# A guarded fallback rewritten as nested loops, and the warm-up matmuls of the opening cut in two

## Chip, cores and metric

One core of one Trainium2 chip. The metric is device time in microseconds of one execution. The kernels compared in one job ran on the same chip in turns.

## The reference

```python
# x, f_logit: (4, 6080, 256); lower_bound: (256,); w_in: (256, 2048); w_out: (2048, 256)
f = lower_bound + (1 - lower_bound) * sigmoid(f_logit)
for t in range(S):                       # a recurrence along the sequence
    h = f[:, t] * h + (1 - f[:, t]) * x[:, t]
    y[:, t] = h
z = y.reshape(B * S, D) @ w_in           # 24320 x 2048
out = (z - tanh(z)) @ w_out
```

## The kernel before

It has two paths. The fast one works on blocks of 512 tokens, uses an approximation of z - tanh(z) that holds for small z, and writes down whether any z was too large (`flags`, summed up into `flag`). Only if one was, a slower path computes everything again.

```python
    fast()
    seen = nc.values_load(flag[:].bitcast(INT32), ...)
    with tc.If(seen != 0):
        general()                       # the path for large h
```

The opening of the fast path has to wait for the first transfers. To get the clock of TensorE up meanwhile, it multiplies zeros (the spares), in four groups of 7, 4, 4 and 2 that stand at fixed places of the instruction order. TensorE is called cold where a matmul of 512 columns takes 0.427 us from start to start, and warm where it takes 0.217; the prediction reads both from the trace.

```python
        def keep_busy(n):
            for _ in range(n):
                nc.tensor.matmul(
                    busy[:], lhsT=zeros.bitcast(BF16)[:, 0:P],
                    rhs=zeros.bitcast(BF16)[:, 0:TB], start=True, stop=True,   # TB = 512
                    skip_group_check=True,
                )
        before = """
            K1.7 df.0 ce.0 ...  sg0.0 cb.0 K1.4
            sg1.0 df.1 ...      F.0.0.0 f0.1 v1.1 f1.1 dx.2 v0.1 K1.4 cw.1
            t.0.0.0 sc0.1 q.0.0.0 F.0.0.1 w.0.0.0 W.3 sc1.1 cr.2 K1.2 a.0.0.0 t.0.0.1
            F.1.0.0 ...                                    # [cut]
```

`K1.n` is a group of n spares, `F.*` the products of the first layer, `sc*` the recurrence on VectorE, `cw.*` the end of a weight's conversion from float64. In the profiles below, `A`, `B`, `D` and `Qa` to `Qd` are the accumulators that a matmul writes, `y` is the recurrence's result, and line 673 holds transposes. The path for large h, before the change, is one loop over time with the four units of 512 hidden columns written out:

```python
        with tc.For_i(0, S, H) as t0:            # 190 steps
            ...                                  # [cut] loads, recurrence
                ps = ps_o.tile([P, D], FP32, name="psO")[0:nb]
                for u in range(NU):              # unrolled: 4 x 12 products
                    for s in range(2):
                        ...                      # 4 products w_in, tanh, 2 products w_out
                nc.scalar.copy(out=osb[0:nb], in_=ps)
```

Of the kernel before, what the change touches and what calls it, by code (L numbers as in the profile page):

```python
# [9 lines left out]
FP32 = mybir.dt.float32  # L10
ALU = mybir.AluOpType
# [4 lines left out]
BF16 = mybir.dt.bfloat16  # L16
PSUM = bass.MemoryType.PSUM
P = 128
# [13 lines left out]
def kernel(  # L32
# [25 lines left out]
    nc = tc.nc  # L58

    B, S, D = x.shape  # L60
    DFF = moe_w_in.shape[1]
    N = B * S
    KC = D // P
    TB = 512
    HB = TB // 2
    NQ = TB // P
    NU = DFF // TB
# [24 lines left out]
    zeros = const.tile([P, TB], FP32, name="zeros")  # L92
# [161 lines left out]
    def fast(ctx):  # L254
# [9 lines left out]
        wpool = ctx.enter_context(tc.tile_pool(name="w", bufs=1))  # L264
# [13 lines left out]
        w_in = [wpool.tile([P, 7, 2 * P], FP32, name=f"w_in{u}") for u in range(NU)]  # L278
        w_out = [wpool.tile([P, 7, 2 * P], FP32, name=f"w_out{u}") for u in range(NU)]
# [366 lines left out]
        for word in around.split():  # L646
            name, u, at = re.fullmatch(r"([a-zA-Z0-9]+)(?:\.(\d))?([+-]\d)?", word).groups()
# [156 lines left out]
        def p_give(j):  # L804
# [29 lines left out]
            t=p_square,  # L834
            q=p_quadratic,
            a=p_factor,
            g=p_shrink,
            w=p_watch,
# [56 lines left out]

        def keep_busy(n):

            for _ in range(n):
                nc.tensor.matmul(
                    busy[:], lhsT=zeros.bitcast(BF16)[:, 0:P],  # L900
                    rhs=zeros.bitcast(BF16)[:, 0:TB], start=True, stop=True,
                    skip_group_check=True,
                )

# [19 lines left out]
        with tc.manual_schedule():  # L924
# [4 lines left out]
                out=lb[:], in_=lower_bound.rearrange("(p k) -> p k", k=KC)  # L929
# [5 lines left out]
                out=om[:], in_=lb[:], func=AF.Identity, scale=-1.0, bias=1.0  # L935
            )
            nc.scalar.activation(out=nom[:], in_=lb[:], func=AF.Identity, bias=-1.0)
            busy = ps_b.tile([P, TB], FP32, name="B", tag="B")
            open_by(before.split())
            for cycle in range(PLAIN + 1, NBLK + 3):  # L940
                for name, u, at in turns:
# [6 lines left out]
                    if u is None:  # L948
                        if final and name == "o1":
                            nc.vector.reduce_max(  # L950
                                out=worst[:], in_=flags[:], axis=mybir.AxisListType.X
# [16 lines left out]
                    if final and (name, u) == ("Qd", NU - 2):  # L968
# [3 lines left out]
                            out=kept[:, 0:2], in_=acc[j, 3][:, :, 0 : sizes[j] // 2]  # L972
                        )

    @with_exitstack
    def general(ctx):


        _, steps, ys, natpool, _, nats, chan = recurrence(ctx)
        wpool = ctx.enter_context(tc.tile_pool(name="w", bufs=1))  # L980
        tpool = ctx.enter_context(tc.tile_pool(name="tpool", bufs=2))
        gpool = ctx.enter_context(tc.tile_pool(name="gpool", bufs=3))
        opool = ctx.enter_context(tc.tile_pool(name="opool", bufs=2))
        ps_h = ctx.enter_context(tc.tile_pool(name="ps_h", bufs=3, space=PSUM))
        ps_o = ctx.enter_context(tc.tile_pool(name="ps_o", bufs=1, space=PSUM))
        w_in = [wpool.tile([P, 2, 2, 2 * P], FP32, name=f"w_in{u}") for u in range(NU)]
        w_out = [wpool.tile([P, 2, 2, D], FP32, name=f"w_out{u}") for u in range(NU)]
        y = wpool.tile([P, KC, B, H], FP32, name="y")
        carry = wpool.tile([P, KC, B], FP32, name="carry")
        nb = B * H  # L990

        def temp(tag, dtype=FP32):
            return tpool.tile([P, 2, 2, HB], dtype, name=tag, tag=tag)

        with tc.manual_schedule():
            nc.vector.memset(carry[:], 0.0)
            for u in range(NU):
                for fetch_w, w in ((fetch_w_in, w_in[u]), (fetch_w_out, w_out[u])):
                    raw = tpool.tile([P, KC * TB], INT64, name="raw", tag="raw")
                    fetch_w(u, raw[:], nc.gpsimd)  # L1000
                    rounding = to_float32(
                        [(w[:].rearrange("p a b c -> p (a b c)"), lambda a: a)], raw[:],
                        lambda n: temp(dict(e="t", m="q", r="th")[n])[:].rearrange(
                            "p a b c -> p (a b c)"
                        ),
                    )
                    for step in ("ce", "cr", "cx", "cm", "cs", "cb", "cw"):
                        rounding[step]()
        with tc.For_i(0, S, H) as t0:
            with tc.manual_schedule():  # L1010
                for s, src in enumerate((f_logit, x)):
                    nat = natpool.tile([P, TB // H, KC * H], FP32, name=("fn", "xn")[s])
                    part = src[:, bass.ds(t0, H), :].rearrange("j b (i c) -> i b j c", i=G)
                    for i in range(G):
                        nc.gpsimd.dma_start(out=nat[i * H : (i + 1) * H, 0:B, :], in_=part[i])
                    nats[ALL, s] = nat
                for step in ("tf", "tx", "sg", "f0", "f1", "v0", "v1"):
                    steps[step](ALL)
                for k in range(KC):
                    for b in range(B):  # L1020
                        nc.vector.tensor_tensor_scan(
                            out=y[:, k, b], data0=chan[ALL, "f", k][:, b * H : (b + 1) * H],
                            data1=chan[ALL, "v", k][:, b * H : (b + 1) * H],
                            initial=carry[:, k, b : b + 1], op0=ALU.mult, op1=ALU.add,
                        )
                nc.vector.tensor_copy(out=carry[:], in_=y[:, :, :, H - 1])
                ps = ps_o.tile([P, D], FP32, name="psO")[0:nb]
                for u in range(NU):
                    for s in range(2):
                        hT = ps_h.tile([P, 2, HB], FP32, name="hT")  # L1030
                        for c in range(2):
                            for k in range(KC):
                                nc.tensor.matmul(
                                    hT[:, c, 0:nb],
                                    lhsT=w_in[u][:, k, s, c * P : (c + 1) * P],
                                    rhs=y[:, k].rearrange("p j b -> p (j b)"),
                                    start=(c == 0 and k == 0),
                                    stop=(k == KC - 1),
                                    skip_group_check=True,
                                )  # L1040
                        h = hT[:, :, 0:nb]
                        t, th, q, small = [
                            temp(n)[:].rearrange("p a b c -> p a (b c)")[:, :, 0:nb]
                            for n in ("t", "th", "q", "small")
                        ]
                        gT = gpool.tile([P, 2, HB], FP32, name="gT")
                        g = gT[:, :, 0:nb]
                        nc.scalar.activation(out=t, in_=h, func=AF.Square)
                        nc.scalar.activation(out=th, in_=h, func=AF.Tanh)
                        nc.scalar.activation(  # L1050
                            out=q, in_=t, func=AF.Square, scale=QA, bias=QB
                        )
                        nc.scalar.activation(
                            out=small, in_=t, func=AF.Relu, scale=-1.0, bias=SMALL
                        )
                        nc.vector.tensor_tensor(out=g, in0=h, in1=th, op=ALU.subtract)
                        nc.vector.scalar_tensor_tensor(
                            out=q, in0=q, scalar=QC, in1=th, op0=ALU.add, op1=ALU.mult
                        )
                        nc.vector.tensor_tensor(out=q, in0=q, in1=t, op=ALU.mult)  # L1060
                        nc.vector.copy_predicated(
                            out=g, mask=small.bitcast(INT32), data=q
                        )
                        for c in range(2):
                            nc.tensor.matmul(
                                ps,
                                lhsT=gT[:, c, 0:nb],
                                rhs=w_out[u][:, s, c, :],
                                start=(u == s == c == 0),
                                stop=(u == NU - 1 and s == c == 1),  # L1070
                            )
                osb = opool.tile([P, D], FP32, name="osb")
                nc.scalar.copy(out=osb[0:nb], in_=ps)
                dst = out.rearrange("(j t) d -> j t d", j=B)[:, bass.ds(t0, H), :]
                for b in range(B):
                    nc.gpsimd.dma_start(out=dst[b], in_=osb[b * H : (b + 1) * H])
# [6 lines left out]
    with tc.If(seen != 0):  # L1083
        general()
# [32 lines left out]
```

## Time and profile before

| | before |
|---|---|
| median of 3 runs | 2331.69 us (2330.61 to 2331.86) |
| span in the profile | 2328.9 us |
| TensorE, VectorE, ScalarE busy | 2318.8, 2121.6, 1802.2 us |

Busy times of a page overlap, so they don't add up to the span. What matters is which engine carries the chain that ended last, and where that engine stands idle. The prediction shows these lines and reads them.

### The profile page before, as it was taken

The numbers are of one execution on the slowest core, as the hardware profiler recorded it, in microseconds if no ns is written. First come the engines' busy times: TensorE is split into PE (matmuls) and PEld (weight loads), VectorE is DVE, ScalarE is ACT, GpSimd is POOL, SyncE is SP. The second block draws the span as 40 slices with busy tenths as digits, with TensorE's granted clock in tenths as the row PEclk, the third lists the DMA queues.
The fourth block names the chain that finished last, engine by engine and source line by source line (L and its number), as shares of the span: only waits on it lengthen the run. The fifth ranks groups of instructions, "written<-read, shape, count | busy, mean of one in ns | idle before, by whom it ended". The sixth has DMA issues, their size and how long they took to land.

```text
span 2328.9 us, 28658 instructions
## 1 busy us (share of the span) xinstructions
PE 2318.8 (100%) x10674; PEld 2024.9 (87%) x10676; DVE 2121.6 (91%) x2451; ACT 1802.2 (77%) x2688; POOL 0.7 (0%) x6
## 2 busy tenths in 40 slices
PE   9999999999999999999999999999999999999998
PEld 6888888888888888888888888888888888888887
DVE  8999899998999989999999999999899998999988
ACT  7677777777777777787777777777777777777775
POOL 0000000000000000000000000000000000000000
PEclk9999999999999999999999999999999999999999
DMA  5211211111111111112111121111211112111101
GB/s 172 64 24 32 41 37 28 28 37 37 37 28 28 38 36 37 28 28 42 32 37 28 28 45 28 37 28 28 46 29 36 28 28 46 31 34 28 28 10 28
DMA packets 296943, 85.00 MB, mean 36 GB/s; under 512 B 289888, under 2 KB 292704, under 8 KB 296800
## 3 DMA queue, kind: packets, MB, share of 16 engines
q1 hardware_dynamic: 296512, 82.87, 16.8%
q8 instruction: 84, 1.38, 0.3%
q14 instruction: 59, 0.48, 0.1%
q10 hardware_dynamic: 288, 0.26, 0.0%
HBM read 58.20 MB, written 24.90 MB: 36 GB/s over the span
## 4 chain that ended last, share of the span: by engine, by line
PE 99%; DMA 0%; SPq 0%; issue 0%; DVE 0%
PE A L392 27%; PE Qa L475 14%; PE D L392 14%; PE Qb L475 14%; PE Qd L475 14%; PE B L392 7%; PE Qc L475 7%; PE Qa L795 1%; PE Qc L795 1%; PE Qb L795 1%; PE A L728 1%; PE D L728 0%; PE Qd L728 0%; DMA xn<-in_x_dram 0%; PE B L728 0%; PE A L561 0%
## 5 line engine op out<-in xcount | busy, mean ns | idle before, releaser
L392 PE MATMUL A<-T,w_in 128*128 128x256 f32 x2208 | 558.8, 379 | 0.0
L392 PEld LDWEIGHTS A<-T,w_in 128*128 128x128 f32 x2208 | 419.5, 190 | 57.0
L436 DVE TENSOR_TENSOR h<-h,q 128x1024 f32<-128x1024 f32 x368 | 437.3, 1218 | 3.1
L430 DVE SCALAR_TENSOR_TENSOR q<-q,t 128x1024 f32<-128x1024 f32 x368 | 439.9, 1215 | 0.0
L423 ACT ACTIVATE q<-t 128x1024 f32<-128x1024 f32 x368 | 382.8, 1053 | 46.5 <-DVE h L436 43.6
L420 ACT ACTIVATE t<-h 128x1024 f32<-128x1024 f32 x368 | 388.7, 1057 | 3.1 <-DVE h L407 0.3
L441 ACT ACTIVATE junk<-t 128x1024 bf16<-128x1024 f32 x368 | 388.3, 1055 | 1.5
L455 DVE TENSOR_TENSOR Tg<-h 128x1024 f32<-128x1024 f32 x368 | 347.9, 945 | 6.3
L475 PE MATMUL Qb<-h,w_out 128*128 128x256 f32 x1472 | 347.7, 379 | 0.0
L475 PEld LDWEIGHTS Qb<-h,w_out 128*128 128x128 f32 x1472 | 279.7, 190 | 38.0
L475 PE MATMUL Qa<-Tg,w_out 128*128 128x256 f32 x736 | 219.0, 379 | 0.0
L475 PE MATMUL Qa<-h,w_out 128*128 128x256 f32 x736 | 218.9, 379 | 0.0
L475 PE MATMUL Qd<-h,w_out 128*128 128x256 f32 x732 | 217.7, 379 | 0.0
L475 PE MATMUL Qd<-Tg,w_out 128*128 128x256 f32 x732 | 217.7, 379 | 0.0
L404 ACT COPY h<-B 128x512 f32<-128x512 f32 x184 | 107.0, 582 | 142.9 <-PE B L392 94.2
L404 ACT COPY h<-A 128x512 f32<-128x512 f32 x184 | 107.1, 582 | 136.6 <-PE A L392 125.2
L407 DVE TENSOR_TENSOR h<-D,r 128x512 f32<-128x512 f32 x184 | 126.8, 689 | 93.2 <-PE D L392 89.4
L407 DVE TENSOR_TENSOR h<-A,r 128x512 f32<-128x512 f32 x184 | 126.2, 686 | 73.9 <-PE A L392 42.1
L404 ACT COPY r<-A 128x512 f32<-128x512 f32 x184 | 107.3, 583 | 105.8 <-PE A L392 105.8
L392 PE MATMUL A<-y,w_in 128*128 128x256 f32 x736 | 188.9, 379 | 0.1
L392 PE MATMUL B<-y,w_in 128*128 128x256 f32 x736 | 188.9, 379 | 0.0
L392 PE MATMUL D<-T,w_in 128*128 128x256 f32 x736 | 188.9, 379 | 0.0
(135 smaller groups left out, 3072.6 us busy)
## 6 DMA issues: line engine op xcount, KB each, us to landing
xn<-in_x_dram SPq DMA_DIRECT2D x184, 128.0 KB, 3.2
fn<-in_f_logit_dram SPq DMA_DIRECT2D x184, 128.0 KB, 3.1
out_dram<-osb SPq DMA_DIRECT2D x180, 128.0 KB, 2.8
raw<-in_moe_w_out_dram SPq DMA_DIRECT2D x8, 512.0 KB, 4.9
raw<-in_moe_w_in_dram SPq DMA_DIRECT2D x7, 512.0 KB, 5.1
out_dram<-osb SPq DMA_DIRECT2D x3, 256.0 KB, 4.1
fn<-in_f_logit_dram SPq DMA_DIRECT2D x1, 512.0 KB, 7.3
xn<-in_x_dram SPq DMA_DIRECT2D x1, 512.0 KB, 8.1
```

Of the source, the lines that this page charges most:

```text
L392: nc.tensor.matmul(ps[:, c], lhsT=w_in[u][:, slot, c * P : (c + 1) * P], rhs=mixes[j][right], start=start and c == 0, stop=True, skip_grou ...
L404: nc.scalar.copy(out=dst, in_=piece(n, bank))
L407: nc.vector.tensor_tensor(out=piece(n, "h")[:, q], in0=piece(n, bank), in1=piece(n, r), op=ALU.add)
L420: nc.scalar.activation(out=half(n, i, "t"), in_=half(n, i), func=AF.Square)
L423: nc.scalar.activation(out=half(n, i, "q"), in_=half(n, i, "t"), func=AF.Square, scale=RA, bias=RB,)
L430: nc.vector.scalar_tensor_tensor(out=q, in0=q, scalar=RC, in1=t, op0=ALU.add, op1=ALU.mult)
L436: nc.vector.tensor_tensor(out=h, in0=h, in1=q, op=ALU.mult)
L441: nc.scalar.activation(out=junk[:, :, :, 0 : st[n]["hb"]], in_=t, func=AF.Relu, bias=-TINY, accum_out=flags[:, 2 * n + i : 2 * n + i + 1],)
L455: nc.vector.tensor_tensor(out=o, in0=a, in1=b, op=ALU.subtract)
L475: nc.tensor.matmul(acc[j, part][:, r, 0 : st[n]["hb"]], lhsT=w_out[u][:, slot, c * P : (c + 1) * P], rhs=piece(n, right)[:, q, c], start=( ...
L728: nc.tensor.matmul(h[c], lhsT=w_in[u][:, 2 * k + s, c * P : (c + 1) * P], rhs=ys[j][:, k, 0:nb], start=k == 0 and (c == 0 or len(banks) == 2),
L795: nc.tensor.matmul(acc[j][i // 2][:, i % 2].rearrange("p (k m) -> p k m", k=2), lhsT=plain[j, u][:, s, c, i * P : (i + 1) * P], rhs=w_out[ ...
```

## The change

Its intent: less code for a path that is normally skipped, and a finer grain for the spares. The two parts don't touch each other. (`TB` is 512 columns, `HB` is 256.)

```diff
         def keep_busy(n):
-            for _ in range(n):
+            for _ in range(2 * n):
                 nc.tensor.matmul(
-                    busy[:], lhsT=zeros.bitcast(BF16)[:, 0:P],
-                    rhs=zeros.bitcast(BF16)[:, 0:TB], start=True, stop=True,
+                    busy[:, 0:HB], lhsT=zeros.bitcast(BF16)[:, 0:P],
+                    rhs=zeros.bitcast(BF16)[:, 0:HB], start=True, stop=True,
                     skip_group_check=True,
                 )
@@ general(): [cut] the weights are loaded and converted in a loop over u as well
-                ps = ps_o.tile([P, D], FP32, name="psO")[0:nb]
-                for u in range(NU):
+            with tc.For_i(0, NU, 1) as u:
+                with tc.manual_schedule():
+                    unit = []
+                    for w in (w_in, w_out):
+                        t = temp("unit")[:].rearrange("p a b c -> p (a b c)")
+                        nc.vector.tensor_copy(out=t, in_=w[:, bass.ds(u, 1)]...)
+                        unit.append(t)
+                    ...                          # [cut] the same 12 products, once
+                    nc.vector.tensor_tensor(
+                        out=total[0:nb], in0=ps, in1=total[0:nb], op=ALU.add
+                    )
```

More of the change, by code (lines that the diff above doesn't have):

```diff
@@ L985, in general @@
         ps_o = ctx.enter_context(tc.tile_pool(name="ps_o", bufs=1, space=PSUM))
-        w_in = [wpool.tile([P, 2, 2, 2 * P], FP32, name=f"w_in{u}") for u in range(NU)]
-        w_out = [wpool.tile([P, 2, 2, D], FP32, name=f"w_out{u}") for u in range(NU)]
+        w_in = wpool.tile([P, NU, 4 * 2 * P], FP32, name="w_in")
+        w_out = wpool.tile([P, NU, 4 * D], FP32, name="w_out")
         y = wpool.tile([P, KC, B, H], FP32, name="y")
         carry = wpool.tile([P, KC, B], FP32, name="carry")
+        total = wpool.tile([P, D], FP32, name="total")
         nb = B * H
@@ L996, in general @@
             nc.vector.memset(carry[:], 0.0)
-            for u in range(NU):
-                for fetch_w, w in ((fetch_w_in, w_in[u]), (fetch_w_out, w_out[u])):
+            nc.vector.memset(total[:], 0.0)
+        with tc.For_i(0, NU, 1) as u:
+            with tc.manual_schedule():
+                for kind, w in enumerate((w_in, w_out)):
                     raw = tpool.tile([P, KC * TB], INT64, name="raw", tag="raw")
-                    fetch_w(u, raw[:], nc.gpsimd)
+                    if kind == 0:
+                        src = moe_w_in.rearrange("(p k) (s u f) -> s u p k f", k=KC, s=2, u=NU)
+                        dst = raw.rearrange("p (k s f) -> p s k f", k=KC, s=2)
+                    else:
+                        src = moe_w_out.rearrange("(s u c m) d -> s u m c d", s=2, u=NU, c=2)
+                        dst = raw.rearrange("p (s c d) -> p s c d", s=2, c=2)
+                    for s in range(2):
+                        nc.gpsimd.dma_start(
+                            out=dst[:, s],
+                            in_=src[s, bass.ds(u, 1)].rearrange("u p k f -> p (u k) f"),
+                        )
                     rounding = to_float32(
-                        [(w[:].rearrange("p a b c -> p (a b c)"), lambda a: a)], raw[:],
+                        [(w[:, bass.ds(u, 1)].rearrange("p u n -> p (u n)"), lambda a: a)],
+                        raw[:],
                         lambda n: temp(dict(e="t", m="q", r="th")[n])[:].rearrange(
@@ L1026, in general @@
                 nc.vector.tensor_copy(out=carry[:], in_=y[:, :, :, H - 1])
-                ps = ps_o.tile([P, D], FP32, name="psO")[0:nb]
-                for u in range(NU):
+            with tc.For_i(0, NU, 1) as u:
+                with tc.manual_schedule():
+                    unit = []
+                    for w in (w_in, w_out):
+                        t = temp("unit")[:].rearrange("p a b c -> p (a b c)")
+                        nc.vector.tensor_copy(
+                            out=t, in_=w[:, bass.ds(u, 1)].rearrange("p u n -> p (u n)")
+                        )
+                        unit.append(t)
+                    wi = unit[0].rearrange("p (k s f) -> p k s f", k=KC, s=2)
+                    wo = unit[1].rearrange("p (s c d) -> p s c d", s=2, c=2)
+                    ps = ps_o.tile([P, D], FP32, name="psO")[0:nb]
                     for s in range(2):
@@ L1034, in general @@
                                     hT[:, c, 0:nb],
-                                    lhsT=w_in[u][:, k, s, c * P : (c + 1) * P],
+                                    lhsT=wi[:, k, s, c * P : (c + 1) * P],
                                     rhs=y[:, k].rearrange("p j b -> p (j b)"),
@@ L1067, in general @@
                                 lhsT=gT[:, c, 0:nb],
-                                rhs=w_out[u][:, s, c, :],
-                                start=(u == s == c == 0),
-                                stop=(u == NU - 1 and s == c == 1),
-                            )
+                                rhs=wo[:, s, c, :],
+                                start=(s == c == 0),
+                                stop=(s == c == 1),
+                            )
+                    nc.vector.tensor_tensor(
+                        out=total[0:nb], in0=ps, in1=total[0:nb], op=ALU.add
+                    )
+            with tc.manual_schedule():
                 osb = opool.tile([P, D], FP32, name="osb")
-                nc.scalar.copy(out=osb[0:nb], in_=ps)
+                nc.vector.tensor_copy(out=osb[0:nb], in_=total[0:nb])
+                nc.vector.memset(total[:], 0.0)
                 dst = out.rearrange("(j t) d -> j t d", j=B)[:, bass.ds(t0, H), :]
```

## The prediction

> **What bounds the kernel now.** I read the page first: busy shares, the chain that ended last, then the opening in order of time, because that is the only executed place that the diff touches. The first fence has whole lines of the page: busy us, share and instruction count of each engine, and the chain by engine.
>
> ```profile
> PE 2318.8 (100%) x10674; PEld 2024.9 (87%) x10676; DVE 2121.6 (91%) x2451; ACT 1802.2 (77%) x2688; POOL 0.7 (0%) x6
> ...
> PE 99%; DMA 0%; SPq 0%; issue 0%; DVE 0%
> ```
>
> TensorE is busy 2318.8 of 2328.9 us and carries 99% of the chain. So only two things can move the time: the work that TensorE does, and the roughly 10 us in which it does nothing, most of them in the first 13 us and the last 6. The table of busy time by stretch puts 13.76 of 17.81 us of TensorE work before 17.81, 82.14 of 82.19 from there to 100, all 2200 of the next 2200, and 22.89 in the last 29. A delay at 17.8 us is therefore handed on whole to the end; nothing later absorbs it.
>
> The spare matmuls are line 899. Here are its group in the view of one line (durations are minimum, median, maximum in ns) and the opening on TensorE in order of time (start, length, what, and in brackets the idle time before it and who ended it).
>
> ```profile
> L899 PEld LDWEIGHTS <-zeros x17: 98/147/152, 1.7 to 17.4; 128*128 128x128 bf16 x17
> L899 PE MATMUL B<-zeros x16: 379/631/634, 1.7 to 17.6; 128*128 128x512 bf16 x16
> ```
>
> ```profile
> 1.70 3.17 PE L899 MATMUL B<-zeros 128*128 128x512 bf16 x7 [1.70 <-DVE ones L926]
> 5.75 0.67 PE L673 MATMUL Qa<-ident,fn 128*128 128x128 f32 x2 [0.88 <-DMA fn<-in_f_logit_dram]
> ...
> 7.50 1.91 PE L899 MATMUL B<-zeros 128*128 128x512 bf16 x4
> 10.53 0.72 PE L673 MATMUL Qa<-ident,fn 128*128 128x128 f32 x4 [1.12 <-DMA fn<-in_f_logit_dram]
> ...
> 12.03 0.72 PE L673 MATMUL Qc<-ident,xn 128*128 128x128 f32 x4 [0.30 <-DMA xn<-in_x_dram]
> 12.58 0.64 PE L673 MATMUL Qd<-ident,xn 128*128 128x128 f32 x4
> 13.06 1.89 PE L728 MATMUL A<-y,w_in 128*128 128x256 f32 x8
> 14.79 1.03 PE L899 MATMUL B<-zeros 128*128 128x512 bf16 x4
> 15.65 1.89 PE L728 MATMUL A<-y,w_in 128*128 128x256 f32 x8
> 17.59 0.38 PE L899 MATMUL B<-zeros 128*128 128x512 bf16 x1
> 17.81 1.88 PE L728 MATMUL Qa<-y,w_in 128*128 128x512 f32 x4
> ```
>
> What to see: the 17 spares (one matmul record is missing; there are 17 weight loads) stand in four groups of 7, 4, 4 and 2. The first two groups end before a wait for a transfer (0.88 and 1.12 us idle after them). The last two stand in a stream with no idle time, so their length counts.
>
> The other part of the diff rewrites the path for large h. Whether it runs is asked of its product line:
>
> ```profile
> nothing on L1033; most used: ['L392', 'L475', 'L404', 'L441', 'L423', 'L455', 'L407', 'L420', 'L182', 'L795', 'L430', 'L436', 'L507', 'L191', 'L728', 'L522', 'L362', 'L214', 'L235', 'L205', 'L673', 'L512', 'L200', 'L491', 'L772']
> ```
>
> With these inputs the flag is zero and the path is branched over.
>
> **What the Trainium skill says.** (1) "TensorE: Matmul & The Clock Gate", Part 1: the array runs at 1.2 GHz until a free-running window of about 3.4 us has been busy, then at 2.4 GHz. The trace agrees: in the group at 7.50, (1.91 - 0.63) / 3 = 0.427 us from start to start for 512 columns, which is 1.2 GHz; at 14.79, (1.03 - 0.38) / 3 = 0.217. The page's granted clock is another thing and reads 1.00 in both. (2) Same page, "Back-to-back issue gap": N / 1.2 ns cold, N / 2.4 + 2.5 ns warm. For 512 this gives 427 and 216, as measured. (3) Same page, "Step-by-step: what each phase is for": the next weight load is pulled ahead and runs beside the matmul before it. The trace agrees in the warm group: four spares at 0.217 us leave no room for a load of 0.098 beside their columns. (4) "Runtime: NRT & Kernel Launch", "Instruction fetch mechanics": a taken branch to a target outside the fetched pages stalls for a fetch. In the trace the branch over the path took 45 to 72 ns on four engines and 367 ns on TensorE, all after the last products.
>
> **The change part by part.**
>
> *Spare matmuls.* 17 x 512 columns become 34 x 256: the same 8704 columns, 17 more weight loads, 17 more matmuls. The first group is cold: 14 x 213 = 2.99 us in place of 7 x 427 = 2.99. Loads of 152 ns fit beside 213 ns. The second is the same: 8 x 213 = 1.71 against 4 x 427 = 1.71. Both end in waits for transfers anyway: 0 us. The last two are warm, and on the path: by the formula of (2), 12 x 109.2 = 1.310 us in place of 6 x 215.8 = 1.295, so +0.016 us. This holds if a load still hides beside 109 ns; the warm loads of zeros took 98 ns, so just so. The trace has one bound for a tighter case: warm transposes of 128 columns of float32, whose columns alone would take 107 ns, are spaced (0.64 - 0.28) / 3 = 0.12 us with float32 loads of 0.21 us. If the new spares ran at 120 to 150 ns instead of 109, the cost would be 12 x 11 to 12 x 41 = 0.13 to 0.49 us. I choose +0.0 to +0.2.
>
> Could shorter groups gain? The matmul at 17.81 also needs the recurrence of VectorE, which runs at 15.26 for 2.45 us, until 17.71. So there are 0.1 us to gain at most.
>
> *The nested loops.* On the executed way this adds and removes nothing: I compared the order of instructions with their waits on each engine of both kernels, and up to the load of the flag VectorE, ScalarE, SyncE and GpSimd have the same instructions and waits (but for buffer numbers), TensorE the same but for the spares. "12 products in the innermost" are never issued. What stays is the jump over a body of another length: in rows of that comparison, 40 become 30 on TensorE, 91 become 61 on VectorE and 10 become 24 on SyncE. A fetch there would mostly hide: SyncE takes its branch at 2324.9, and its closing waits sit on the last store until 2327.2. Estimate 0, at worst some tenths of a us.
>
> Sum: 2331.7 + 0.1 = 2331.8 us.
>
> **The rivals.** *A, a clock that warms a window later.* If the monitor counts the 17 loads as pauses, or if the window's phase falls badly, the array may still be cold at 10.5 us. For it: warm-up now comes between 9.4 and 10.5, after a busy stretch of only 3.7 us, hardly longer than one window. Against it: the busy and idle stretches keep their places and lengths. Cost: the eight transposes at 12.03 go from 0.12 to 0.21 (0.7 us), the eight matmuls at 13.06 from 0.216 to 0.427 (1.7 us), so about +2.4 us: 2334. *B, weight loads become the bound of the spares* (the 0.13 to 0.49 us above): 2332.2 at most. *C, smaller pieces let real products in earlier, a gain.* Against it: TensorE takes its instructions in the order written and the columns are as many, and VectorE's 17.71 caps it: 2331.6. *D, the jump costs a fetch on the ending chain:* +1 us at most, since the store's wait of 1.7 us covers it. *E, the path for large h runs after all:* ruled out by the empty view, as the flag's arithmetic is unchanged.
>
> **Range and chances.** None of these exceeds 2.4 us, 0.1%, while 2% is 47 us. The three runs before lie within 1.25 us. Adding that spread and a little for another session to the terms: 2329.8 to 2334.4. Within 2%: 0.985; the rest is for something not in the profile, rather slower (0.010) than faster (0.005).
>
> **What would show it.** Line 899 with about 34 loads and matmuls of 256 columns; first two groups spaced 0.213, last two about 0.109; the matmul on Qa at 17.8 to 18.0; nothing on the lines of the path; TensorE busy about 2319. Spacing of 0.12 or more in the last two groups is B; transposes at 10.5 and 12.0 spaced 0.21 is A; a late start of the closing waits is D. I would be wrong if any group changed beyond 20 us.

## The result

| | before | after |
|---|---|---|
| median of 6 runs | 2330.70 us (2330.50 to 2331.86) | 2330.39 us (2329.86 to 2331.35) |
| TensorE busy in the profile | 2318.8 us | 2319.0 us |

The ratio is 0.9998, with a 95% interval of 0.9985 to 1.0011: the same. A ratio here is the mean time of one kernel's fast runs over the mean of the other's fast runs of the same rounds, so it is not quite the ratio of the medians.

The page of the kernel after, busy times and the chain by engine:

```profile
PE 2319.0 (100%) x10693; PEld 2027.1 (87%) x10693; DVE 2122.2 (91%) x2451; ACT 1802.3 (77%) x2688; POOL 0.7 (0%) x6
...
PE 99%; DVE 0%; DMA 0%; ACT 0%; issue 0%; ACTq 0%
```

The spares of the kernel after (durations are minimum, median and maximum, in ns):

```profile
L899 PEld LDWEIGHTS <-zeros x34: 97/147/151, 1.7 to 17.5; 128*128 128x128 bf16 x34
L899 PE MATMUL B<-zeros x34: 272/418/421, 1.7 to 17.6; 128*128 128x256 bf16 x34
```

Its opening on TensorE in order of time (start, length in us, what, idle time before):

```profile
1.70 3.17 PE L899 MATMUL B<-zeros 128*128 128x256 bf16 x14 [1.70 <-DVE ones L926]
...
7.99 1.91 PE L899 MATMUL B<-zeros 128*128 128x256 bf16 x8
...
14.69 1.04 PE L899 MATMUL B<-zeros 128*128 128x256 bf16 x8
15.56 1.89 PE L728 MATMUL A<-y,w_in 128*128 128x256 f32 x8
17.29 0.60 PE L899 MATMUL B<-zeros 128*128 128x256 bf16 x4
17.73 1.88 PE L728 MATMUL Qa<-y,w_in 128*128 128x512 f32 x4
```

The groups last what they lasted before: 3.17 and 1.91 us in the cold part to the hundredth, 1.04 against 1.03 us in the warm part. The spacing, from start to start, is (1.91 - 0.42) / 7 = 0.213 us cold and (1.04 - 0.27) / 7 = 0.110 us warm. The first matmul on Qa comes at 17.73 us (17.81 before). The path for large h again left no instruction in the trace: the view of its product line answers that nothing lies on it.

The last transposes of TensorE, before and after, give a sharper measure than the time does:

```profile
2322.50 0.38 PE L578 MATMUL D<-ident,C 128*128 128x128 f32 x2
```

```profile
2322.43 0.38 PE L578 MATMUL D<-ident,C 128*128 128x128 f32 x2
```

From the first matmul on Qa to the end of these it is 2322.50 + 0.38 - 17.81 = 2305.07 us before and 2322.43 + 0.38 - 17.73 = 2305.08 after. These two executions are the same to about 0.01 us over 99% of the span. What differs between them lies in the first 20 us or in the last 6.

### The profile page after: what moved, and what is told of

Its sections match the earlier page's. It is cut to its first block, busy times and chain, and to the rows that moved or that the text cites. A ratio compares the mean times of both kernels' runs of the same rounds, so it can differ in the third digit from the quotient of the medians.

```text
span 2328.7 us, 28694 instructions
## 1 busy us (share of the span) xinstructions
PE 2319.0 (100%) x10693; PEld 2027.1 (87%) x10693; DVE 2122.2 (91%) x2451; ACT 1802.3 (77%) x2688; POOL 0.7 (0%) x6
## 4 chain that ended last, share of the span: by engine, by line
PE 99%; DVE 0%; DMA 0%; ACT 0%; issue 0%; ACTq 0%
PE A L392 27%; PE Qa L475 14%; PE Qb L475 14%; PE D L392 14%; PE Qd L475 14%; PE Qc L475 7%; PE B L392 7%; PE Qa L795 1%; PE Qc L795 1%; PE Qb L795 1%; PE A L728 1%; PE D L728 0%; PE Qd L728 0%; PE B L728 0%; DMA lb<-in_lower_bound_dram 0%; PE A L561 0%
## 5 line engine op out<-in xcount | busy, mean ns | idle before, releaser
L392 PE MATMUL D<-y,w_in 128*128 128x256 f32 x736 | 188.9, 379 | 0.0
```

The lines of the kernel that those rows point to most:

```text
L392: nc.tensor.matmul(ps[:, c], lhsT=w_in[u][:, slot, c * P : (c + 1) * P], rhs=mixes[j][right], start=start and c == 0, stop=True, skip_grou ...
```

## The experiments

All are built from the kernel after, unless said otherwise. The runs scatter by 1 to 4 us, so ratios carry intervals of 0.13 to 0.15%; differences below 3 us are read from the traces.

### Each part alone

`path_only`: the new path, with the spares of before.

```diff
-            for _ in range(2 * n):            # 256 columns
+            for _ in range(n):                # 512 columns
```

> Only the path for large h is rewritten; the spare matmuls are those of before. Theory (the path is branched over, so it costs nothing): same time as before within 0.1%, nothing on the path's lines, the branch over it 45 to 72 ns on four engines and about 367 ns on TensorE, the closing waits of SyncE ending at 2327 to 2328. Rival (the two parts of the change cancel each other, the path's shape costs or saves a fetch at the jump): 1 to 3 us apart from before, with a longer branch or a late start of the closing waits.

Measured: 2330.30 us against 2331.03, ratio 0.9998 (0.9984 to 1.0012). The branch over the path took 45 to 72 ns on four engines and 367 ns on TensorE, as it did before the change. SyncE's last closing wait started at 2327.5 us, in the expected stretch. The interval is too wide to rule out the rival's 1 us, but neither a longer branch nor a late start of the closing waits is there. A shorter end is taken up under "The jump over the path".

`spares_only`: the kernel before, with the new spares.

> Only the spare matmuls are in pieces of 256 columns; the path is that of before. Theory (same columns, weight loads hidden): +0.016 us, not to be told from before; spacing 0.213 us in the first two groups, 0.109 in the last two; matmul on Qa starts at 17.7 to 18.3. Rival (weight loads or the smaller pieces show): spacing of 0.12 us or more in the last two groups and +0.13 to +0.5 us, or a cold array at 10.5 and +2 us.

Measured: 2331.00 us against 2331.03, ratio 0.9997 (0.9984 to 1.0011). The time is as the theory has it. The profile brought a surprise. Here is the opening on TensorE in this run:

```profile
6.01 0.47 PE L673 MATMUL Qa<-ident,fn 128*128 128x128 f32 x2 [1.14 <-DMA fn<-in_f_logit_dram]
...
7.19 1.04 PE L899 MATMUL B<-zeros 128*128 128x256 bf16 x8
10.50 0.71 PE L673 MATMUL Qa<-ident,fn 128*128 128x128 f32 x4 [2.28 <-DMA fn<-in_f_logit_dram]
...
11.98 1.10 PE L673 MATMUL Qc<-ident,xn 128*128 128x128 f32 x4 [0.28 <-DMA xn<-in_x_dram]
12.87 1.06 PE L673 MATMUL Qd<-ident,xn 128*128 128x128 f32 x4
13.73 2.74 PE L728 MATMUL A<-y,w_in 128*128 128x256 f32 x8
...
19.34 1.88 PE L728 MATMUL Qa<-y,w_in 128*128 128x512 f32 x4
```

TensorE was warm already at 7.19 (eight spares in 1.04 us, not 1.91) and cold again from 12 us: the transposes at 12.87 take 1.06 us where the kernel before took 0.64. The matmul on Qa came at 19.34 us, 1.5 later than in the kernel before. The instructions that were executed are those of the kernel after, which had the matmul at 17.73. So the same instructions can meet the clock in different phases. Whether the kernel before can as well is asked below.

### How much of the spares is on the path

`late_x8`: the two warm groups eight times as long.

```diff
-  dx.2 v0.1 K1.4 cw.1 ...   sc1.1 cr.2 K1.2 a.0.0.0
+  dx.2 v0.1 K1.32 cw.1 ...  sc1.1 cr.2 K1.16 a.0.0.0
```

> The changed kernel with the two warm groups of spares eight times as long: 96 matmuls of 256 columns in place of 12. Theory (these groups stand on the path that sets the end, and nothing later absorbs a delay): 84 x 0.109 = +9.2 us, less the 0.1 us by which TensorE now leads the recurrence, so about 2339.6 us, 0.4% longer; TensorE busy 2328. Rival (the opening is bounded by loads and VectorE, and spares are hidden, or later slack absorbs them): less than 3 us longer.

Measured: 2340.03 us against 2331.03, ratio 1.0038 (1.0022 to 1.0053), that is +9.0 us by the medians. The lines of this run that carry it:

```profile
14.65 7.15 PE L899 MATMUL B<-zeros 128*128 128x256 bf16 x64
...
26.86 0.59 PE L728 MATMUL Qa<-y,w_in 128*128 128x512 f32 x1
...
2331.55 0.38 PE L578 MATMUL D<-ident,C 128*128 128x128 f32 x2
```

The matmul on Qa moved by 26.86 - 17.73 = 9.13 us, and 2331.55 + 0.38 - 26.86 = 2305.07 us lie between it and the end of the last matmul, as in the two kernels above. Nothing later absorbed any of the delay. This is shown.

`late_none`: without these two groups.

```diff
-  dx.2 v0.1 K1.4 cw.1 ...   sc1.1 cr.2 K1.2 a.0.0.0
+  dx.2 v0.1 cw.1 ...        sc1.1 cr.2 a.0.0.0
```

> The changed kernel without the two warm groups of spares. Theory (VectorE's recurrence ends at 17.7 and holds the first matmul on Qa, so the 1.31 us of spares only fill a wait): gain of 0.1 us at most, an idle time of about 1.3 us on TensorE before 17.8 us, split between the waits for the weight at 15.4 and the recurrence at 17.7. Rival (spares on the path cost what they last): 1.31 us shorter. If the shorter busy time lets the clock fall, it is longer by up to 2 us, with float32 matmuls of 256 columns spaced 0.427 after 17.7.

Measured: 2330.71 us against 2331.03, ratio 0.9997 (0.9983 to 1.0011): neither 0.1 nor 1.31 us can be told apart by the time. In the profile the clock fell again as in the run above, and the 16 first products ran without a pause, so the idle time that the theory expected did not come up; TensorE was itself the slower one.

```profile
18.03 1.88 PE L728 MATMUL Qa<-y,w_in 128*128 128x512 f32 x4
```

```profile
15.73 2.46 DVE L235 TENSOR_TENSOR_SCAN y<-f,y,v 128x512 f32<-128x512 f32 x2
```

The matmul on Qa came at 18.03 us, 1.31 earlier than the 19.34 of the other run with a cold spell, which is what 12 spares of 0.109 us last. That the two numbers agree so well is in part chance: the first products had started 0.24 us earlier too (13.49 against 13.73), and the other three profiles with a cold spell have this matmul at 19.01 to 19.57 us. So it fits the rival in such an execution, roughly. At the last transposes 1.22 of the 1.31 us were left.

The two lines show something else: the first matmul on Qa ran before the recurrence had ended, at 15.73 + 2.46 = 18.19 us. It reads only the first of the two halves of `y` (`ys[j][:, k]` in the kernel); the second matmul, 0.43 us later, reads the other. So the theory's wait was put on the wrong matmul, and its limit of 0.1 us was too low: in the kernel before, from the end of the recurrence (17.71) to the second matmul on Qa (17.81 + 0.43) it is about 0.5 us. How much there is to gain in an execution without the cold spell stays open.

`early_none`: without the two groups at the start.

```diff
-  K1.7 df.0 ce.0 ...  cb.0 K1.4
+  df.0 ce.0 ...       cb.0
```

> The changed kernel without the two cold groups of spares (22 of its 34). Theory (they only warm the clock before 10.5 us; transfers bound the rest): the array is still cold when the transposes and the first products come, so transposes spaced 0.213 and products of 256 columns spaced 0.427 for up to one window of 3.4 us; +1.5 to +3 us. Rival (transfers and VectorE hide the cold stretch, or the transposes at 5.8 us start the window alone): within 0.5 us of before.

Measured: 2330.98 us against 2331.03, ratio 0.9999 (0.9985 to 1.0013). The medians differ by 0.05 us, as the rival had it; the interval reaches from 3.5 us shorter to 3.0 longer, so that it does not rule out most of the expected 1.5 to 3 us. The trace shows the cold stretch that the theory describes (the transposes at 10.2 to 13.7 spaced 0.21 us), and the matmul on Qa at 18.95 us, 1.2 later than in the kernel after. But the kernels with the early spares reach 19 us and more in some executions too. What the early spares gain on average is below what these rounds resolve; the theory's size is not borne out.

### A finer cut

`pieces_128`: 68 spares of 128 columns.

```diff
-            for _ in range(2 * n):   # busy[:, 0:HB], rhs [:, 0:HB]
+            for _ in range(4 * n):   # busy[:, 0:P],  rhs [:, 0:P]
```

> The changed kernel with its spares cut once more: 68 matmuls of 128 columns, the same columns again. If a weight load of zeros needs its 98 ns before the next one can start, the last two groups run at about 0.1 us apiece, 24 x 0.1 = 2.4 us in place of 1.31, and the time is +1.1 us; the cold groups stay at 0.107 or go to 0.15. If loads overlap one another, spacing is about 0.056 us and the time stays the same.

The spares of this run, as a group and in the third of their places:

```profile
L899 PEld LDWEIGHTS <-zeros x68: 97/98/151, 1.7 to 19.5; 128*128 128x128 bf16 x68
```

```profile
16.44 1.06 PE L899 MATMUL B<-zeros 128*128 128x128 bf16 x16
```

Measured: 2331.37 us against 2331.03, ratio 0.9998 (0.9984 to 1.0011). The second expectation held. Sixteen spares in 1.06 us, the last of them 0.22 long, are spaced (1.06 - 0.22) / 15 = 0.056 us, although each has a weight load of 0.098 us. So the duration of a load in the trace is not the time for which it keeps the next one waiting. With pieces of 256 columns the margin was not "just so", as the prediction had it, but at least a factor of two.

### Does the kernel before have the cold spell too?

`before_look1` and `before_look2`: the kernel before, unchanged, one profile each.

> The kernel before, unchanged, for another profile. The two kernels that differ only in code that is never run gave two openings: in one the array was cold until 10.5 us and warm from then on, in the other warm at 6 us and cold again from 12 to 15. Theory (the phase of a free-running window decides, not the size of the pieces): the kernel before shows the second kind too in about half of its executions, transposes at 12.0 spaced 0.21 and the matmul on Qa at 19 instead of 17.8. Rival (spares of 512 columns keep the clock better): it never does.

> A second such look at the kernel before, with the same two expectations: about half of the executions cold again at 12 us, or none.

In the first look (2332.33 us) TensorE stayed cold until about 14.5 us, with the matmul on Qa at 19.50. In the second (2332.08 us) it was warm at 6, cold from 12 to 15, with that matmul at 19.01. The second by stretches of one us; the columns are the stretch, its length, busy time and instructions of five engines, then granted clock, share and GB/s of the transfers:

```profile
6.00:7.00 1.00, 0.94 (x7) 0.91 (x8) 0.73 (x2) 1.00 (x3) 0.00 (x0) 1.00 0.93 332
12.00:13.00 1.00, 1.00 (x7) 1.00 (x6) 0.11 (x1) 0.97 (x3) 0.00 (x0) 0.50 1.03 370
14.00:15.00 1.00, 1.00 (x4) 0.82 (x3) 1.00 (x2) 0.00 (x0) 0.00 (x0) 0.50 1.40 171
```

The granted clock reads 0.50 in the cold spell. So spares of 512 columns don't protect from it: the rival falls. Among the twelve profiles with the short programs (the last experiment's two included) five had the cold spell at 12 us, one of the kernel before and four with smaller pieces; five were warm throughout from 8.8 to 10.7 us on, two with 512 columns and three with 256; two stayed cold until 14.6 or 14.7, one of the kernel before and `early_none`. Twelve are too few to say that the frequencies are equal.

The clock records of these traces also show what the cold spell follows. In all five it lasts 3.41 us, after 6.83 us (twice as long) at full clock. The first two lines are of `spares_only`: the 3.41 us before its spell, and the spell. The third is of the kernel before, which was warm from 9.48 us on and stayed so:

```profile
8.62:12.03 3.41, 1.24 (x9) 1.11 (x9) 3.41 (x8) 1.41 (x3) 0.00 (x0) 1.00 1.07 381
12.03:15.44 3.41, 3.41 (x13) 3.03 (x14) 1.53 (x4) 2.19 (x4) 0.00 (x0) 0.50 1.26 246
```

```profile
9.48:12.89 3.41, 2.06 (x15) 1.93 (x16) 2.65 (x5) 2.23 (x4) 0.00 (x0) 1.00 1.07 378
```

In the 3.41 us before each of the five spells TensorE was busy for 1.24 to 1.52 us. In every other such stretch of the warm openings, counted from where the clock rose, it was busy for 2.06 us or more, and stayed warm. That fits a clock that is set anew every 3.41 us by how busy TensorE has been, at a phase that differs from one execution to the next: the idle time between 8 and 12 us falls into one stretch or is split between two. No run sets the phase, so this is read from twelve traces and not shown by experiment.

### The jump over the path

`no_branch`: no load of the flag, no branch, no path (right for these inputs only); run a second time as `no_branch_again`.

```diff
     fast()
-    seen = nc.values_load(flag[:].bitcast(INT32), ...)
-    with tc.If(seen != 0):
-        general()
```

> The changed kernel without the load of the flag, the branch and the whole path for large h (right for these inputs only). Theory (the jump lies beside the wait for the last store): SyncE's closing waits start about 0.8 us earlier, the last store lands when it did, and the time is the same within 0.3 us. Rival (the jump or the fetch of code behind it is on the ending chain): 0.8 us or more shorter.

> The kernel without flag load, branch and path, once more. In its first profile the closing stretch after the last matmul took 4.23 us, where ten kernels with the branch had 5.1 to 6.0, because the last store landed 3.3 us after that matmul and not 4.1 to 5.0; the start was 0.25 us earlier, as four register moves of GpSimd were gone. If the branch delays the last store: 4.2 us again, and about 1 us shorter than before over the rounds. If the landing of a store just varies: 5 to 6 us, and within 0.5 us of before.

Measured: 2329.86 us against 2331.03, ratio 0.9994 (0.9981 to 1.0007), and the second time 2329.77 against 2331.93, ratio 0.9990 (0.9977 to 1.0004). Both intervals hold 1, so the time leaves it unclear, but both profiles show the same two differences. First, the spares start at 1.45 us instead of 1.70, and four register moves of GpSimd at the start are gone. Second, the end is shorter. SyncE's closing waits, in the first of these runs and in the kernel after (first and last start):

```profile
L1136 SPq EVENT_SEMAPHORE  x7: 17/28/28, 2323.7 to 2326.7; - x7
```

```profile
L1142 SPq EVENT_SEMAPHORE  x14: 17/28/28, 2325.0 to 2328.6; - x14
```

The last transpose ended at 2322.13 + 0.38 = 2322.51 in the former and at 2322.81 in the latter, so the last wait starts 4.2 us after it without the branch and 5.8 with it. From the last transpose to the end of the span it was 4.23 and 4.24 us without the branch, and 5.1 to 6.0 in the ten short programs with it. The last two stores, in the transfers of `no_branch` and of the kernel after (the last number is the median time from issue to landing, in us):

```profile
out_dram<-osb SPq DMA_DIRECT2D x2, 256.0 KB, 2.4
```

```profile
out_dram<-osb SPq DMA_DIRECT2D x2, 256.0 KB, 4.0
```

The theory that the jump hides beside the wait for the last store falls: the store itself landed later where there is a branch, 4.1 to 5.0 us after the last transpose in place of 3.3. How that comes about, with a store that is issued before the branch, is open; no run here separates the load of the flag, the jump, the seven further closing waits, and the transfers of instructions (three or four packets around the last stores with the branch, one without).

Nor is it clear that it costs both kernels alike. From the last transpose to the end it was 5.9 to 6.0 us in the four profiles with the old path, and 5.1 to 5.9 in the six with the rewritten one. The rewritten path may have made the end some tenths of a us shorter; no run tests this, and the times are too coarse for it.

### What the rewritten path costs where it does run

`large_after` and `large_before`: the threshold below zero, so that the path runs after the fast one. The outputs are right.

```diff
-TINY = 0.03
+TINY = -1.0
```

> The changed kernel with the threshold set below zero, so that the path for large h runs after the fast one (the output is written twice and right). It measures what the rewritten path costs when it does run. Theory: 190 steps of 4 inner turns, each with its barriers and copies of the weights; estimate 2330 us plus 190 x 40 to 100 us, 10 to 21 ms. If the whole came out near 2330 us the path would not have run.

> The kernel before with the threshold set below zero: its own path for large h runs after the fast one. To be set beside the changed kernel's 16667.86 us. Theory: one loop of 190 steps without inner turns has a quarter of the barriers and no copies of the weights, so it costs a half or less of the changed path: 2330 us plus 190 x 20 to 40 us, 6 to 10 ms. Rival (the products or VectorE bound both): within 15% of the changed one.

Measured, one run each of unknown state: 16667.86 us with the nested loops, 14435.32 with the single one. Less the 2331 us of the fast path that is 14337 against 12104 us, or 75.5 against 63.7 us for each of 190 steps. The time of the nested version lies in the expected 10 to 21 ms. For the single loop the expectation of "a half or less" was wrong. The rival's number held (13% below the changed kernel), but not its reason: TensorE was busy for 48 and 52% of the two spans and VectorE for 40 and 36%, so neither was the bound all the time. The two groups of the nested version that the other one does not have, and the wait at the head of each inner turn:

```profile
L1096 DVE TENSOR_TENSOR total<-psO,total 128x256 f32<-128x256 f32 x760 | 322.8, 425 | 1396.8 <-PE psO L1089 1396.8
...
L1046 DVE COPY unit<-w_in 128x1024 f32 x760 | 522.7, 688 | 678.6 <-PEq L1041 678.6
...
L1046 DVE COPY unit<-w_out 128x1024 f32 x760 | 521.4, 686 | 0.0
```

Copies (522.7 + 521.4), additions (322.8) and the wait for the turn (678.6) come to 2046 us, beside a difference of 2233. That looks like an account, but it leaves out the products: their busy time was 5893.6 against 5452.4 us, 441 us more, at a mean granted clock of 0.609 against 0.668. With them the terms come to 2487 us, more than the difference, so some of this work runs beside other work. Which parts make the difference is open, as I ran no version without the copies. With these inputs none of it is ever paid.

## Why the prediction was right

The measured 2330.39 us lies in the range, and the forecast "same" held.

- **The path is never executed: right.** Nothing of it is in the trace, and alone it left the time unchanged.
- **Same columns, same time for the spares: right.** 0.213 us cold and 0.110 warm were measured, 0.213 and 0.109 forecast, and TensorE's busy time is 2319.0 us.
- **A delay at 17.8 us is handed on whole: right,** and shown by the eightfold groups: 9.1 us at the start, 9.0 in the time.
- **Rival B, weight loads as the bound: mis-sized.** The prediction compared the duration of a load, 98 ns, with the spacing of 109. The runs show a spacing of 56 ns with the same loads.
- **Rival A, a later or falling clock: the mechanism was right and tied to the wrong thing.** It was left out of the sum and taken for a matter of the change. It came up in both kernels: with all the spares in place, the matmul on Qa stood at 17.0 to 17.8 us in warm openings and at 19.0 to 19.6 in cold ones, up to 1.8 us later than in the first two profiles, where the prediction had 2.4. Which of the timed runs had it is not known, so that it left no difference between the two medians is in part luck.
- **"The granted clock ... reads 1.00 in both": true for that trace, and misleading.** The record falls to 0.50 in the cold spell of other executions. The first, cold stretch of every execution stands there as 1.00, though its spacing is that of half the clock.
- **Rival C, 0.1 us at most to gain: the limit was read from the wrong matmul.** In `late_none` the first matmul on Qa ran before the recurrence had ended; only the second needs it, which leaves about 0.5 us and not 0.1. With a cold spell about 1.2 us were gained. But the new spares have the same columns, so nothing was gained by the change, as forecast.
- **Rival D, the jump is covered by the last store's wait: wrong in its reason,** as the store lands 0.8 to 1.7 us later with the flag load, the branch and the path in the program. An effect on the comparison was not seen in the times; some tenths of a us are possible. A smaller slip: the branches were not all after the last products, as GpSimd took its branch at 2321.0 us.
- **The predicted time itself** was 1.4 us above the measured one. The reference run of the same chip was 2330.70 us and not the 2331.69 that it started from, which is 1.0 of it. Its six runs begin with the three known before.

## What to carry to other kernels

Ask first of each part of a diff whether its lines are in the trace: here the body of the fallback that was branched over left no instruction in the trace, and what the program paid was at its two ends: 0.25 us at the start and 0.9 to 1.8 at the end, with the flag load and the branch in it. Then look for a stretch that is the same in every execution (here 2305.07 to 2305.17 us in twelve profiles) and read small differences from the trace at its two ends, since times that scatter by some us cannot show them. Idle-time fillers are worth what the clock makes of them; if the warm-up falls on different phases from run to run, judge them over several profiles and not from one.

## What the Trainium skill lacked or had wrong

- "TensorE: Matmul & The Clock Gate", Part 1, gives the rule of no idle gaps above about 3.4 us. Here the longest idle times before the five cold spells were 1.94 to 2.40 us; what they had in common is 3.41 us with TensorE busy for only 1.24 to 1.52.
- The same page's Part 4 says that the full clock doesn't engage for transposes, which don't count as busy in the same way. Here it did: in `before_look1` TensorE ran nothing but float32 transposes from 11.14 to 14.55 us, busy for 3.07 us, and the products from 14.75 us on were spaced (1.89 - 0.38) / 7 = 0.216 us, as in the warm groups.
- The same page names the trace's clock events unreliable and does not say how to read the stretch before the first of them. Here the granted clock read 1.00 in the first cold stretch, where 512 columns took 0.427 us, and 0.50 in a later one.
- The same page's section "LDWEIGHTS (loading the stationary operand)" gives P / 1.2 ns, 107 for 128 columns. Loads of bfloat16 zeros took 98 ns warm and 147 to 152 cold, and followed each other every 56 ns beside matmuls of 128 columns; the section gives a duration and no spacing.
- "Runtime: NRT & Kernel Launch", section "Instruction fetch mechanics", speaks of the stall of a taken branch. Here the branch took 45 to 367 ns, and the closing stretch was 5.1 to 6.0 us with it and 4.2 without, the last store landing later; no page has this.
